# The last two table products made unit by unit, with a new order for the first stage

## The chip, the cores and the metric

The kernel runs on one core of one Trainium2 chip. The metric is the time of one execution on the device, in microseconds (us). The time before is the median of three runs; beside it there is one execution that the hardware profiler recorded.

## The reference

The model has two kinds of layers, each used twice: a long convolution along the sequence (2048 positions, 512 channels), and an attention over 8 dilated neighbours.

```python
x = A_u
x = x + _A_ref(_layernorm(x), ...)
x = x + _B_ref(_layernorm(x), ...)
x = x + _A_ref(_layernorm(x), ...)
x = x + _B_ref(_layernorm(x), ...)

def _A_ref(u, ...):
    logdA = dt * (A_re + 1j * A_im)                      # 512 channels x 128 modes
    l = arange(L).astype(A_re.dtype)                     # the lags, 0 to 2047
    P = exp(logdA[:, :, None] * l[None, None, :])
    K = einsum("dn,dnl,dn->dl", Cc, P, dB).real          # the filter of each channel
    y = irfft(rfft(u padded) * rfft(K padded))[:L]       # the convolution, by FFT
    return y + u * Dskip
```

The change lies in the first convolution layer, where the filter K is made and the convolution is run.

## The kernel before

The first stage (`kernel_and_first_conv`) makes K without ever forming P. A power of exp(logdA) for any lag is a product of two factors, one from a table Y (20 lags) and one from a table X (32 lags, multiples of 8). TensorE contracts X against Y over the 128 modes, which gives K at all lags that are wanted. In the code the first factor of each matmul is X, with Btab beside it (the second half of the same complex product for the upper 16 lags); these are the first factor's tables.

The 512 channels are cut into 8 units of 64. The tables are made on VectorE (DVE) for one or two units at a time: `CHUNKS` says unit 0 alone, 1 alone, 2 with 3, 4 with 5, 6 alone, 7 alone. For a chunk, `table_ops` first copies a seed into Y (line 423) and into X (line 428). It then doubles the tables step by step: y0, y1, y2, a, b, d, e for Y, and x1, x2, x3, x4 for X. A step is a complex multiplication: two products (lines 467 or 469, and 476 into the scratch Tscr) and an addition (482). x4 has no addition: its second product goes to Btab, and TensorE adds it up. There is room in the tables for two units; unit u may overwrite the place of unit u - 2 when that has been contracted.

For each unit, `contract` does the rest: TensorE contracts the tables into psk (line 485), psk is cast to kq (829), TensorE selects the rows (pk, 840), and pk is cast to KT (847). Two units make one group of 128 channels (dc). `k_fft` takes KT of a group through the two steps of the Fourier transform: products with FK into ps_s and Z (874, 877), a turn of Z into zt (by DMA, line 887, or by TensorE, 910 and 914), products with C2 into xp (894), and a cast to sp_k (905). `u_fft` does the same for the input: F1 in place of FK, with sp_u as the result. A copy of sp_u with its halves swapped is made by DMA or by DVE (961). DVE multiplies sp_u by sp_k into pa (969), and TensorE goes back (vp, VT, ps_y, lines 983, 986, 1005) to X (1009). A stored sp_k goes to kt_scratch for the second convolution layer.

The order of all that work is not found at run time. The code lists the operations in a `Plan`, with a choice between ways for some (which engine evacuates a buffer, or whether a turn goes by DMA). `Plan.run` then issues them in the order of a row of numbers, `ORDERS`, one row for each of the kernel's stages. Each engine executes what it gets in that order and waits at its head; nothing overtakes. An operation's costs in the code (`pl.op("V", 2 * us, ...)`) were used to find the rows and have no effect here.

SyncE (SP) issues most DMA transfers, in order as well. Early in the stage it loads the input X, turns it by DMA into xT (line 703), from which TensorE makes gram matrices (712, 716) and DVE the layer norm (721 on), and loads the constants and weights: F (F1) for `u_fft`, FK, C2, IC, F1T, and wv and wqk for the attention layer. The mean is taken out of these weights by `centred`, through ps_wc, ps_wm and wm.

Of the kernel before, what the change touches and what calls it, by code (L numbers as in the profile page):

```python
# [231 lines left out]
def load_params(nc, pp, prm):  # L232
# [14 lines left out]

GATES = (13,)
ORDERS = [
# [106 lines left out]
def moved(pl, nc, name, us, slow, fn, *after, **needs):  # L356
    return pl.either(name, lambda: pl.op("A", us, lambda: fn(nc.scalar.copy), *after, **needs),
                     lambda: pl.op("V", slow, lambda: fn(nc.vector.tensor_copy), *after, **needs))
# [156 lines left out]
def table_ops(pl, nc, T, u, n, seeds, free, fixed, casts):  # L515
    e = T.elements

    def step(what, *after):
        out = []
        for v, m in ((u, 1), (u + 1, 1)) if n == 2 and what == "x3" else ((u, n),):  # L520
            us, key = e(m, what) / 1920 + 0.069, ("sc", v, what)
            a = pl.op("V", 2 * us + (0.06 if what in ("y1", "y2", "x1", "x2") else 0), lambda v=v, m=m: T.times(v, m, what), *after, casts[T.POWER[what]], take=[] if what == "x4" else key)
            if what != "x4":
                a = pl.op("V", us, lambda v=v, m=m: T.add(v, m, what), a, drop=key)
            out.append(a)
        return out
    y = moved(pl, nc, ("seed", u), 0.15 + 0.1 * n, 0.08 + 0.066 * n, lambda copy: T.seed(copy, u, n), seeds, free)
    x = moved(pl, nc, ("second", u), 0.15 + 0.1 * n, 0.08 + 0.066 * n, lambda copy: T.second(copy, u, n), casts[3], free)
    for what in ("y0", "y1", "y2", "a", "b", "d", "e"):
        y = step(what, y)  # L530
    x = step("x1", x, fixed)
    for what in ("x2", "x3", "x4"):
        x = step(what, x)
    return [y, x]


def vt(n):
# [222 lines left out]
def kernel_and_first_conv(nc, tc, C, prm, x2d, const, kt_dram, eps, Wt):  # L760
    with ExitStack() as es:
# [4 lines left out]
        T = Tables(nc, tc, es, M)  # L766
# [13 lines left out]
        pl = Plan(psk=2, kq=2, psA=3, Z=2, zt=3, KT=2, lk=NKT, xc=NXC, xs=NXS, lads=4, pa=2, VT=1, sc=2)  # L780
# [18 lines left out]
        box, Td, Cd, Kd, Sd, Fd, Xq, Pd, Rd = {}, {}, {}, {}, {}, {}, {}, {}, {}  # L799
# [131 lines left out]
        def u_fft(dc):  # L931
            dsl = slice(dc * DCH, (dc + 1) * DCH)
            fs = spectrum("u", dc, 0, 4, lambda j, r: [(F1[:, j, r, :], columns(X, j, dc))], lambda jq: [marks["xn", jq], L["F1"], free], None)

            def residual():
                nc.sync.dma_start(columns(X, slice(0, NJ), dc), xv[:, :, dsl])
            Rd[dc] = pl.op("S", 0.7, residual, *fs, lag=5.2)

        def k_fft(dc, b0, nb):
            c0, c1 = b0 * 32, (b0 + nb) * 32  # L940

            def mats(j, r):
                x = box.get(("KT", dc))
                todo = [(late["FK"][:, i, r, :] if x else None, x and x[:, s, c0:c1]) for s, i in pairs[j]]
                if j == 0 and r == 0:
                    todo.append((C["onesr"][:], D2[:, dc * DCH + c0:dc * DCH + c1]))
                return todo
            last = [("KT", dc)] if b0 + nb == 4 else []
            spectrum("k", dc, b0, nb, mats, lambda jq: [Rd["FK", jq], L["onesr"], L["D2"], marks["k0"], *[Kd[u] for u in range(dc * 2, dc * 2 + 2) if (u % 2) * 2 < b0 + nb]], last)
# [15 lines left out]
        def product(dc, c):  # L965
            def go():
                s, t, k = box.pop(("u", dc, c)), box.pop(("swap", dc, c)), box["k", dc, c]
                pr = box["pa", dc, c] = lp.tile([128, 2, 1024], BF, name="pa", tag="pa", bufs=2)
                nc.vector.tensor_tensor(pr[:], box["U"][:, s:t + 1:t - s], k[:].unsqueeze(1).to_broadcast([128, 2, 1024]), ALU.mult)  # L969
                box["xc"].append(s)  # L970
                box["xs"].append(t)
            return pl.op("V", 1.14, go, Sd["swap", dc, c], Pd["k", dc, c], take=[("pa", dc, c)], drop=[("xc", dc, c), ("xs", dc, c), ("lk", "kt", dc, c)])
# [100 lines left out]
        for u in range(8):  # L1073
            for u0, n in CHUNKS:
                if u0 == u:
                    o = table_ops(pl, nc, T, u0, n, marks["seeds"], [Cd[x - 2] for x in range(u0, u0 + n) if x > 1], marks["fixed"], marks["casts"])
                    for x in range(u0, u0 + n):
                        Td[x] = o
            contract(u)
            dc = u // 2  # L1080
            if dc == 3:
                k_fft(3, u % 2 * 2, 2)
            elif u % 2:
                k_fft(dc, 0, 4)
            if u % 2:
                for c in range(4):
                    inverse(dc, c, product(dc, c))
                final(dc, 4 if dc == 3 else 8)
                if dc < 3:
                    u_fft(dc + 1)  # L1090
# [912 lines left out]
```

## Time and profile before

| | |
|---|---|
| median of 3 runs | 422.04 us (421.99 to 422.74) |
| the profiled execution, its time | 420.84 us |
| its span in the profile | 419.1 us |
| DVE busy over the span | 390.4 us (93%) |
| PE (TensorE) busy over the span | 354.5 us (85%) |
| ACT (ScalarE) busy over the span | 325.5 us (78%) |
| first stage, to the last X written back | 160.1 us |

All times in rows of the timeline are us from the span's start: first the start, then the duration, the engine, the line, the operation, output<-inputs with shapes, and in brackets the idle time before it with what ended it. A row with x2 or more merges instructions that follow each other; the next row's start minus this row's start is what an instruction costs an engine that is never idle. A row of waits has the total, the number of times, and the longest. DVE is VectorE, ACT is ScalarE, PE is TensorE's matmuls, PEld its weight loads.

### The profile page before, as it was taken

The page shows a single profiled execution, that of the slowest core. Times are in us where ns is not written, and L with a number is a line of the kernel's source. Part 1 is how long each engine was busy: PE and PEld are TensorE (multiplying, and loading weights), DVE is VectorE, ACT ScalarE, POOL GpSimd, SP SyncE. Part 2 cuts the span into 40 slices and gives each one's busy share as a digit, 9 for nine tenths or more (in the row PEclk, how much of TensorE's full clock was granted, in tenths as well). Part 3 has the DMA queues.
Part 4 walks back from the last instruction along what each step waited for, and adds up shares of the span by engine and source line. Part 5 has one row for each costly group of instructions (what it writes and reads, how often), then busy time and mean ns, then how long its engine had stood idle before and what let it go on. Part 6 is the DMA issues. An engine that isn't in the chain of part 4 may idle for free. (4 is left out here: it accounts for less than half of the span.)

```text
span 419.1 us, 13750 instructions
## 1 busy us (share of the span) xinstructions
PE 354.5 (85%) x5906; PEld 226.5 (54%) x5906; DVE 390.4 (93%) x643; ACT 325.5 (78%) x534; POOL 29.0 (7%) x99
## 2 busy tenths in 40 slices
PE   1367777887999989999975999899999999966995
PEld 1342555665787865446642444678864456632452
DVE  6999999799999897989999999999999999999994
ACT  6899999899899964678964589999966788762630
POOL 2000000000000200010100203020000010000321
PEclk9998899999999999999999899999999999995899
DMA  7998447987869977002334277799951000352396
GB/s 216 199 207 290 168 82 123 170 180 155 179 140 161 206 165 120 19 2 70 88 92 88 49 163 159 156 178 186 208 112 40 20 0 2 89 134 56 50 180 139
DMA packets 104914, 52.80 MB, mean 126 GB/s; under 512 B 84043, under 2 KB 96476, under 8 KB 104598
## 3 DMA queue, kind: packets, MB, share of 16 engines
q1 hardware_dynamic: 99014, 45.24, 49.9%
q0 software_dynamic: 3376, 5.37, 6.6%
q10 hardware_dynamic: 2464, 1.31, 1.1%
q8 instruction: 46, 0.75, 0.8%
q14 instruction: 14, 0.11, 0.1%
HBM read 19.30 MB, written 6.29 MB: 61 GB/s over the span
## 5 line engine op out<-in xcount | busy, mean ns | idle before, releaser
L1706 DVE TENSOR_TENSOR prod<-VX,L 128x512 bf16<-128x512 bf16 (+2 forms) x72 | 75.4, 1099 | 0.8 <-DMA VX<-VX 0.3
L1530 DVE TENSOR_TENSOR prod<-qT,kT 128x4096 bf16<-128x4096 bf16 (+1 forms) x40 | 72.3, 1855 | 0.5 <-ACT kT L1436 0.3
L877 ACT CAST Z<-ps_s 128x1024 bf16<-128x1024 f32 (+1 forms) x36 | 32.6, 944 | 1.5 <-PE ps_s L874 1.4
L1818 PE MATMUL ps_o<-wo_t,oT 128*32 128x512 bf16 x512 | 33.6, 395 | 0.0
L1485 PE MATMUL ps_v<-wv,U 128*128 128x256 bf16 x256 | 31.6, 272 | 1.7 <-ACT VX L1496 1.0
L1431 PE MATMUL ps_qk<-U,wqk 128*128 128x512 bf16 x128 | 30.3, 380 | 0.7 <-ACT qT L1436 0.7
L1496 ACT ACTIVATE VX<-ps_v,rs 128x256 bf16<-128x256 f32 x64 | 26.7, 471 | 3.8 <-PE ps_v L1485 3.0
L1485 PEld LDWEIGHTS <-U 128*128 128x128 bf16 x256 | 24.5, 97 | 9.6 <-issue 5.1
L1450 PE MATMUL ps_qk<-U,wqk 128*128 128x512 bf16 x128 | 28.8, 379 | 0.8 <-ACT X L1212 0.8
L1541 PE MATMUL Lp<-prod,sb_bones 128*32 128x512 bf16 x256 | 22.4, 412 | 5.7 <-DVE prod L1530 5.7
L1748 ACT CAST ot<-po 128x1024 bf16<-128x1024 f32 (+1 forms) x15 | 14.4, 985 | 14.3 <-PE po L1721 10.8
L1721 PE MATMUL po<-prod,sb_ident 32*32 32x512 bf16 x768 | 17.1, 428 | 7.7 <-DVE prod L1706 7.5
L969 DVE TENSOR_TENSOR pa<-sp_u,sp_k 128x2048 bf16<-128x2048 bf16 x16 | 19.2, 1221 | 4.0 <-ACT sp_k L905 2.8
L894 PE MATMUL xp<-zt,sb_C 128*128 128x512 bf16 x64 | 18.8, 379 | 4.7 <-ACT zt L914 2.2
L1818 PEld LDWEIGHTS <-oT 128*32 128x32 bf16 x512 | 13.3, 100 | 14.2 <-issue 3.8
L1431 PEld LDWEIGHTS <-wqk 128*128 128x128 bf16 x128 | 11.8, 98 | 17.0 <-issue 4.8
L1450 PEld LDWEIGHTS <-wqk 128*128 128x128 bf16 x128 | 12.4, 98 | 15.2 <-issue 1.1
L874 PE MATMUL ps_s<-KT,FK 128*128 128x128 bf16 (+1 forms) x360 | 18.9, 209 | 1.5 <-ACT KT L847 1.1
L1174 DVE TENSOR_TENSOR pa<-xc,Kt 128x2048 bf16<-128x2048 bf16 x16 | 18.9, 1217 | 0.6 <-PE vp L1186 0.3
L874 PEld LDWEIGHTS <-FK 128*128 128x128 bf16 x360 | 17.3, 98 | 3.3 <-issue 2.2
L905 ACT CAST sp_k<-xp 128x1024 bf16<-128x1024 f32 x16 | 16.2, 1029 | 2.3 <-PE xp L894 1.7
L983 PE MATMUL vp<-sb_IC,pa 128*128 128x128 bf16 x256 | 16.8, 219 | 1.4 <-ACT sp_k L905 0.7
(231 smaller groups left out, 862.4 us busy)
## 6 DMA issues: line engine op xcount, KB each, us to landing
kt_scratch<-sp_k SPq DMA_DIRECT2D x16, 256.0 KB, 3.1
Kt<-kt_scratch POOLq DMA_DIRECT2D x16, 256.0 KB, 5.9
sp_u<-sp_u SPq DMA_DIRECT2D x22, 128.0 KB, 3.2
X<-in_A_u_dram SPq DMA_DIRECT2D x8, 256.0 KB, 6.3
X<-in_A_u_dram SPq DMA_DIRECT2D x4, 512.0 KB, 5.2
Kt<-kt_scratch SPq DMA_DIRECT2D x8, 256.0 KB, 4.3
VX<-VX SPq DMA_DIRECT2D x4, 448.0 KB, 3.9
VX<-VX SPq DMA_DIRECT2D x4, 336.0 KB, 3.4
```

What stands on the lines that cost most here:

```text
L874: nc.tensor.matmul(ps[:, r, 0:n // 4, jj * 4:(jj + 1) * 4], w, x, start=(k == 0), stop=(k == len(todo) - 1))
L877: nc.scalar.copy(box["Z", kind, dc, b0][:, 0:n // 4, :, jq * 16:(jq + 1) * 16].rearrange("p g r k -> p r g k"), box.pop(("s1", kind, dc, j ...
L969: nc.vector.tensor_tensor(pr[:], box["U"][:, s:t + 1:t - s], k[:].unsqueeze(1).to_broadcast([128, 2, 1024]), ALU.mult)
L1174: nc.vector.tensor_tensor(pr[:], x[:].unsqueeze(1).to_broadcast([128, 2, 1024]), box.pop(("kt", dc, c))[:], ALU.mult)
L1431: nc.tensor.matmul(ps[:], wqk[:, ct, f0:f0 + 128], XT[:, ct // 2, 4 * s:4 * s + 4, ct % 2, :], start=(ct == 0), stop=(ct == 3))
L1450: nc.tensor.matmul(box[name][:, k * 512:k * 512 + 512], wqk[:, ct, f0:f0 + 128], XT[:, ct // 2, 4 * s:4 * s + 4, ct % 2, :], start=(ct == ...
L1485: nc.tensor.matmul(ps[:, jj].rearrange("p t h d -> p (t h d)"), XT[:, ct // 2, j + jj, ct % 2, :], wv[:, ct, fp * 256:(fp + 1) * 256], sta ...
L1496: nc.scalar.activation(out, ps, ACT.Identity, scale=r)
L1530: nc.vector.tensor_tensor(pr[:], windows(q, 0, 2), windows(kT[fp][:, a:a + n2, col(w):col(w) + 1024], -DIL * 128, 2), ALU.mult)
L1541: nc.tensor.matmul(Lp[r0:r0 + 32, w // 4, :], bones[:, w % 4 + k, :], pr[:, k, f2 - a, hb * 512:(hb + 1) * 512], start=(n == 1 and k == 0) ...
L1706: nc.vector.tensor_tensor(p2[:].rearrange("p w j t d h -> p w (j t) d h"), windows(v, -DIL * 256, taps), l.to_broadcast([128, taps, nj * 2 ...
L1818: nc.tensor.matmul(ps[r:r + 32], lhsT, rhs, start=(ft == -1 or ft == 0 and not res), stop=(ft == 3), skip_group_check=True)
```

## The change

In `table_ops`, x4 of a chunk of two units was one step of two instructions. It is now a step for each unit, x3 and x4 of a unit as a pair (x3 was made unit by unit before, too). A unit's contraction then waits for its own x4 alone, and no longer for that of its neighbour; it still waits for the Y table of both. The number of operations in the plan changes, and the order of the first stage is a new row, found by a search.

```diff
-    def step(what, *after):
-        out = []
-        for v, m in ((u, 1), (u + 1, 1)) if n == 2 and what == "x3" else ((u, n),):
-            us, key = e(m, what) / 1920 + 0.069, ("sc", v, what)
-            a = pl.op("V", 2 * us + (0.06 if what in ("y1", "y2", "x1", "x2") else 0), lambda v=v, m=m: T.times(v, m, what), *after, casts[T.POWER[what]], take=[] if what == "x4" else key)
-            if what != "x4":
-                a = pl.op("V", us, lambda v=v, m=m: T.add(v, m, what), a, drop=key)
-            out.append(a)
-        return out
+    def step(v, n, what, *after):
+        us, key = e(n, what) / 1920 + 0.069, ("sc", v, what)
+        extra = 0.06 if what in ("y1", "y2", "x1", "x2") else 0
+        a = pl.op("V", 2 * us + extra, lambda: T.times(v, n, what), *after, casts[T.POWER[what]], take=[] if what == "x4" else key)
+        return a if what == "x4" else pl.op("V", us, lambda: T.add(v, n, what), a, drop=key)
...
     for what in ("y0", "y1", "y2", "a", "b", "d", "e"):
-        y = step(what, y)
-    x = step("x1", x, fixed)
-    for what in ("x2", "x3", "x4"):
-        x = step(what, x)
-    return [y, x]
+        y = step(u, n, what, y)
+    for what in ("x1", "x2"):
+        x = step(u, n, what, x, fixed if what == "x1" else [])
+    return [[y, step(v, 1, "x4", step(v, 1, "x3", x))] for v in range(u, u + n)]
...
                     for x in range(u0, u0 + n):
-                        Td[x] = o
+                        Td[x] = o[x - u0]
```

Of the order's row only the first numbers:

```diff
-    "1 3 7 2 8 5 9 10 19 24 11 14 30 12 13 34 31 35 45 49 20 21 25 26 28 23 38 166 239 39 47 42 55 160 48 56 67 57 59 61 "
+    "242 1 3 2 7 8 9 24 25 164 26 5 10 11 162 12 236 14 27 13 19 30 20 31 21 34 35 45 23 47 48 67 42 38 49 59 68 43 166 "
```

In the row of the attention stage one number (52) moves four places on; no engine's instructions come in another order by it.

The new row also takes other ways for some operations of the first stage. DVE's instructions in the kernel go from 645 to 652: four more for x4; one more normalisation of X (4 for 3), two more seeds of Y (one of 256 elements, one of 128), one kq cast, and one more swap (two copies); one quad step (`stepped`, now four ACTIVATEs on ACT), one MYB (now on ACT) and one write-back of X (now on ACT) fewer. ACT gives up one normalisation, two seeds and one kq cast.

Lines after line 528 have numbers that are 5 lower in the new kernel. Three places follow, before and after each.

DVE at the end of the tables of units 2 and 3, before:

```order
L476 TENSOR_TENSOR Tscr<-Ytab,MSB 128x512
L469 TENSOR_TENSOR Xtab<-Xtab,MSA 128x128x32
L476 TENSOR_TENSOR Btab<-Xtab,MSB 128x4096
L482 TENSOR_TENSOR Ytab<-Ytab,Tscr 128x64x2x4
L969 TENSOR_TENSOR pa<-sp_u,sp_k 128x2048 x2
L961 COPY sp_u<-sp_u 64x1024 x2
L428 COPY Xtab<-MX_73 128x128x2
```

The same place after:

```order
L476 TENSOR_TENSOR Btab<-Xtab,MSB 128x2048
L482 TENSOR_TENSOR Ytab<-Ytab,Tscr 128x64x2x4
L469 TENSOR_TENSOR Xtab<-Xtab,MSA 128x64x32
L476 TENSOR_TENSOR Btab<-Xtab,MSB 128x2048
L956 COPY sp_u<-sp_u 64x1024 x2
L824 CAST kq<-psk 128x40x8
L964 TENSOR_TENSOR pa<-sp_u,sp_k 128x2048 x2
L423 COPY Ytab<-cb_91 128x64x4
L428 COPY Xtab<-MX_73 128x128x2
```

The two Btab rows are the two units' x4. The swap of sp_u moved ahead of pa, and a kq cast and a seed were added on DVE.

ACT around the first casts of sp_k, before:

```order
L905 CAST sp_u<-xp 128x1024
L914 COPY zt<-pt 128x1024 x2
L905 CAST sp_k<-xp 128x1024 x2
L829 CAST kq<-psk 128x40x8 x2
L905 CAST sp_u<-xp 128x1024
L829 CAST kq<-psk 128x40x8
L905 CAST sp_k<-xp 128x1024
```

The same place after:

```order
L900 CAST sp_u<-xp 128x1024
L909 COPY zt<-pt 128x1024 x2
L824 CAST kq<-psk 128x40x8
L900 CAST sp_k<-xp 128x1024 x2
L900 CAST sp_u<-xp 128x1024
L900 CAST sp_k<-xp 128x1024
L824 CAST kq<-psk 128x40x8 x2
```

The first kq cast (unit 2) moved ahead of the first sp_k.

SP's queue from the last turns of X to the weights (c_F is the constant F1), before:

```order
L703 DMA_TRANSPOSE xT<-X 128x8x128 x2
L144 DMA sb_ident<-c_ident 128x128
L703 DMA_TRANSPOSE xT<-X 128x8x128
L1068 DMA wv<-in_B_wqkv_dram 128x4x512
L144 DMA sb_C_155<-c_C 128x128
L144 DMA sb_onesr<-c_onesr 2x128
L144 DMA sb_F_153<-c_F 128x4096
L1068 DMA wqk<-in_B_wqkv_dram 128x4x1024
```

The same place after:

```order
L698 DMA_TRANSPOSE xT<-X 128x8x128 x3
L144 DMA sb_F_153<-c_F 128x4096
L698 DMA_TRANSPOSE xT<-X 128x8x128
L144 DMA sb_IC<-c_IC 128x256
L698 DMA_TRANSPOSE xT<-X 128x8x128 x2
L144 DMA sb_F1T<-c_F1T 128x4096
L1063 DMA wv<-in_B_wqkv_dram 128x4x512
L1063 DMA wqk<-in_B_wqkv_dram 128x4x1024
```

F moved ahead of the last three turns, and F1T, which was issued after FK, ahead of both weights.

46 rows, old and new, of the table ORDERS are left out of this document.

## The prediction

> **What bounds the kernel now.** The order table that is new belongs to the first stage, so I read that stage alone: first the busy time by stretches (0 to 160.1 us ends with the last X written back), then VectorE's (DVE's) waits from 60 to 160 us, then its timeline. Columns of the stretches: length, then busy time of PE, PEld, DVE, ACT, POOL, the granted clock, DMA share, GB/s.
>
> ```profile
> 0.00:75.00 75.00, 44.46 (x949) 30.61 (x950) 70.72 (x164) 69.05 (x103) 2.12 (x11) 0.95 0.74 183
> 75.00:105.00 30.00, 25.11 (x605) 19.88 (x604) 27.03 (x47) 27.62 (x36) 0.00 (x0) 1.00 0.83 169
> 105.00:136.50 31.50, 30.11 (x922) 24.93 (x919) 29.46 (x79) 28.68 (x42) 0.00 (x0) 1.00 0.81 158
> 136.50:160.10 23.60, 21.07 (x439) 16.90 (x434) 19.72 (x29) 19.01 (x26) 2.10 (x4) 1.00 0.79 178
> ```
>
> DVE is busy 147 of 160 us and ACT 144. Both run in order, so the stage lasts about DVE's work plus what DVE waits. Those waits are few:
>
> ```profile
> DVE pa L969 <- ACT sp_k L905: 2.8, 2, 2.6
> DVE Xtab L428 <- PE psk L485: 0.7, 2, 0.5
> DVE pa L969 <- PE vp L983: 0.6, 1, 0.6
> DVE Ytab L423 <- PE psk L485: 0.3, 1, 0.3
> ```
>
> The largest is behind the x4 product of units 2 and 3:
>
> ```profile
> 70.17 2.28 DVE L469 TENSOR_TENSOR Xtab<-Xtab,MSA 128x4096 bf16<-128x4096 bf16 x1
> 72.37 2.28 DVE L476 TENSOR_TENSOR Btab<-Xtab,MSB 128x4096 bf16<-128x4096 bf16 x1
> 74.57 0.42 DVE L482 TENSOR_TENSOR Ytab<-Ytab,Tscr 128x512 bf16<-128x512 bf16 x1
> 77.57 2.36 DVE L969 TENSOR_TENSOR pa<-sp_u,sp_k 128x2048 bf16<-128x2048 bf16 x2 [2.58 <-ACT sp_k L905]
> 79.97 0.86 DVE L961 COPY sp_u<-sp_u 64x1024 bf16<-64x1024 bf16 x2
> 81.03 0.30 DVE L428 COPY Xtab<-MX 128x256 bf16<-128x256 bf16 x1 [0.21 <-PE psk L485]
> ...
> 135.29 1.22 DVE L476 TENSOR_TENSOR Btab<-Xtab,MSB 128x2048 bf16<-128x2048 bf16 x1
> ```
>
> DVE has nothing in hand from 74.99 to 77.57: the product pa needs sp_k, and the next tables need the contraction (psk) of both units. Unit 7's table is ready at 136.51, and 23.6 us of chain follow it.
>
> **The change part by part: work.** x4 for two units at once is two instructions of 4096 elements. Split, it is four of 2048, as units 0 and 1 have it now:
>
> ```profile
> 42.87 1.22 DVE L469 TENSOR_TENSOR Xtab<-Xtab,MSA 128x2048 bf16<-128x2048 bf16 x1
> 44.00 1.22 DVE L476 TENSOR_TENSOR Btab<-Xtab,MSB 128x2048 bf16<-128x2048 bf16 x1
> 45.14 0.28 DVE L482 TENSOR_TENSOR Ytab<-Ytab,Tscr 128x256 bf16<-128x256 bf16 x1
> ```
>
> Start to start, 2048 elements take 1.135 us and 4096 take 2.20, so 8 x 1.135 - 4 x 2.20 = +0.28 us. The other moves between engines are priced by these rows (the second fence is ACT's):
>
> ```profile
> 11.19 1.29 DVE L551 TENSOR_TENSOR quad<-t,dtf 128x512 f32<-128x512 f32 x2
> 13.01 0.42 DVE L642 TENSOR_SCALAR MYB<-LAM 128x512 bf16<-128x512 f32 x1
> 13.34 0.69 DVE L682 TENSOR_TENSOR lads<-sq 128x512 f32<-128x512 f32 x1
> ...
> 50.63 0.40 DVE L229 TENSOR_SCALAR X<-X,ln_rstd_a,ln_nb_a 128x512 bf16<-128x512 bf16 x1
> 50.95 0.45 DVE L847 CAST KT<-pk 128x288 bf16<-128x288 f32 x1
> 51.32 0.40 DVE L229 TENSOR_SCALAR X<-X,ln_rstd_a,ln_nb_a 128x512 bf16<-128x512 bf16 x1
> ...
> 150.91 1.23 DVE L1009 CAST X<-ps_y 128x1024 bf16<-128x1024 f32 x1
> ```
>
> ```profile
> 3.44 1.28 ACT L568 ACTIVATE e_mag<-raw_A_re,dtf 128x128 f32<-128x128 bf16 x4
> ...
> 9.11 0.58 ACT L610 COPY LAM<-ptq 128x512 f32<-128x512 f32 x1 [1.41 <-PE ptq L603]
> ...
> 13.76 0.58 ACT L616 CAST cb<-ptq 128x512 bf16<-128x512 f32 x1 [1.60 <-PE ptq L603]
> ```
>
> Ahead of unit 7's table DVE loses one quad step (-0.61) and one MYB (-0.33), and gains one normalisation (+0.32), the seeds and one kq cast. The trace has no kq cast on DVE: KT, 288 elements instead of 320, takes 0.37 start to start and a 512-element pass 0.6 (quad), so I take +0.41, near KT. One more seed of 128 elements and one of 256 are bounded by nothing and 0.30 each (row 81.03); I take 0.32 together. With the split: +0.39. ACT takes the quad step as four ACTIVATEs, 1.28 by the e_mag row. They lie in the 1.41 it waits before LAM, and since this quad is ready sooner, the 1.60 before cb goes too.
>
> **Dependent pairs.** The order also decides whether an instruction follows directly on the one whose output it reads:
>
> ```profile
> 108.54 0.22 DVE L476 TENSOR_TENSOR Tscr<-Ytab,MYB 128x128 bf16<-128x128 bf16 x1
> 108.79 0.23 DVE L482 TENSOR_TENSOR Ytab<-Ytab,Tscr 128x128 bf16<-128x128 bf16 x1
> ...
> 117.90 0.22 DVE L476 TENSOR_TENSOR Tscr<-Ytab,MYB 128x128 bf16<-128x128 bf16 x1
> 118.03 0.42 DVE L482 TENSOR_TENSOR Ytab<-Ytab,Tscr 128x512 bf16<-128x512 bf16 x1
> ```
>
> The same product lets its own addition start after 0.25 us (108.54), but an addition of another step after 0.13 (117.90). I count 20 direct product-to-addition pairs and 14 addition-to-product pairs before, 11 and 13 in the new order: 10 fewer at 0.11 to 0.12, -1.1 us (none to -1.2). The Trainium skill, "VectorE: DVE Perf Modes", section "The DRAIN you can't avoid", says that the pipe empties after every operation and that waits between chained operations cost nothing extra. By it this term would be 0 and the sum below 1.1 us worse; the rows above disagree with it. Work in all: 0.39 - 1.1 = -0.7 us at unit 7's table.
>
> **Waits.** Before, DVE waits 2.58 and 0.21 in the rows above and 0.47 (0.7 less 0.21), 0.3 and 0.6 by the table: 4.2 us that the new order can reach. In the new order x4 of unit 2 ends some 2.3 us before that of unit 3, PE contracts unit 2 meanwhile, and DVE has a swap (0.86) and the kq cast (0.41) ahead of pa. But pa still needs sp_k:
>
> ```profile
> 72.99 1.95 ACT L914 COPY zt<-pt 128x1024 bf16<-128x1024 bf16 x2
> 75.61 1.93 ACT L905 CAST sp_k<-xp 128x1024 bf16<-128x1024 f32 x2 [0.68 <-PE xp L894]
> ```
>
> ACT gets there 1.2 us sooner: the early waits of 1.41 and 1.60 end, less 1.8 of work taken over (the quad step's 1.28 and 0.5 for MYB, near cb's 0.58). The new kq cast on ACT stands ahead of sp_k and waits for unit 2's contraction, which PE starts after its xp: that gives half of it back, and pa starts near 77.0. I leave 1.2 of the 2.58 in place. The rest, with the contraction of unit 3 some 2 us earlier and unit 6's table seeds no longer behind both contractions, should go: -2.7 us (bounds 0 and -4.2).
>
> **New waits.** SP's loads are rearranged: F (1 MB) now goes ahead of the last three transposes of X, and F1T (1 MB) ahead of the weights wv and wqk. PE works in order, so behind wqk's product ps_wm stands the first contraction, and behind that DVE's first KT:
>
> ```profile
> 30.24 0.30 PE L716 MATMUL gram<-xT 128*32 128x32 bf16 x16
> 37.76 1.02 PE L1024 MATMUL ps_wm<-wqk,mones 128*128 128x512 bf16 x4 [2.84 <-DMA wqk<-in_B_wqkv_dram]
> 45.48 1.01 PE L485 MATMUL psk<-Ytab,Xtab 128*64 128x40 bf16 x32 [0.65 <-DVE Ytab L482]
> ```
>
> ```profile
> 33.59 0.68 DVE L721 TENSOR_TENSOR own<-gram,sb_block 128x512 f32<-128x512 f32 x1
> ```
>
> ```profile
> 22.00:24.00 2.00, 0.00 (x0) 0.00 (x0) 2.00 (x8) 2.00 (x4) 0.00 (x0) 1.00 0.89 70
> ...
> 32.00:34.00 2.00, 2.00 (x6) 0.74 (x5) 2.00 (x7) 2.00 (x4) 0.00 (x0) 1.00 1.01 370
> ```
>
> A megabyte at 370 GB/s is 2.8 us. The gram ends at 30.5 and DVE takes it at 33.59, so that cover is 3 us, or 2 with DVE a microsecond ahead: F costs 0 to 0.8. From wqk's landing (37.7) to KT (50.95) are 13.2 us, only 0.65 of them the wait above, so a delay of wqk shows at KT nearly in full. From 22 to 24 us the DMA engines move only 70 GB/s, room that F would use, so I expect wqk within half a microsecond of now: +0.3 (0 to 3.5).
>
> **Tail.** Behind unit 7's table DVE loses an X write-back (-1.15) and gains a swap (+0.86); ACT gains the write-back late in the chain (0.97, as the sp_k cast of the same size). I take +0.5 (0 to 1.3).
>
> Sum: -0.7 - 2.7 + 0.3 + 0.5 = **-2.6 us**. From 160 us on no engine's order differs, so it should arrive whole. The profiled execution took 420.84 (span 419.1); 418.24 follows. The median, 422.04, lies 1.20 above it: **419.4**.
>
> **Rivals.**
> 1. *The weights come late: slower.* If F finds no room, wqk lands 2.8 us later, at 40.5, and KT follows 12.5 to 13.2 us on, at 53.0 to 53.7, while DVE, 0.7 us ahead, asks for it near 50.3. DVE then stands 2.7 to 3.4 us, and the gram adds up to 0.8. With 3.4 + 0.8 for the 0.3 the sum is +1.3: 423.3. It turns slower once the early stall passes 2.9 us. For it: the share of 1.01 in the row at 32 us. Against: the 70 GB/s of the row at 22. The Trainium skill, "DMA: Bandwidth & Descriptors", section "Queues, rings and completion order", has descriptors of a ring consumed in order, which speaks for the transposes waiting behind all of F; no run here shows it yet. Chance 0.14.
> 2. *The wait is only renamed.* kq on ACT holds sp_k, DVE stands at its own kq cast, pa starts at 77.6 or after, and the later waits stay by half: -0.7 - 1.3 + 0.3 + 0.5 = -1.2, 420.8. For it: PE's contraction stands behind an xp that waits for ACT. Chance 0.14.
> 3. *ACT becomes the bound.* ACT takes over the quad step, MYB and an X write-back (1.28 + 0.5 + 0.97) and gives up a normalisation, seeds and a kq cast (some 1.5): 1.2 us more, at 144 busy of 160. If its other 16 us, spent waiting, shrink by no more than that, the end stays: 422.0. Chance 0.10.
>
> **Chances and range.** My forecast has the remaining 0.62. A measurement tells 0.2%, 0.84 us, from no change. Faster: 0.62 + 0.14 = 0.76; within: 0.07 of rival 3; slower: 0.14 + 0.03 = 0.17. The range runs from the full waits and no new ones (-0.7 - 4.2 = -4.9, 417.2) to most of rival 1 (+1.0, 423.0).
>
> **What would show it.** Right: the wait of pa on sp_k near 76 us under 1.5 us, tables of units 4 and 5 begun by 79.9, unit 7's Btab done by 133.5, X written back by 157.5, and later stages shifted alike. Wrong: DVE idle at "own" or at the first KT, PE's wait for wqk above 3.9 us, sp_k later than 75.6, or ACT busy without gaps after 136 us.

## The result, and the profile after

| | before | changed | ratio, 95% interval |
|---|---|---|---|
| median, 17 runs of each | 421.99 us | 419.37 us | 0.9935, 0.9916 to 0.9953 |
| again, beside later experiments, 11 and 6 runs | 421.62 us | 419.55 us | 0.9948, 0.9928 to 0.9968 |
| profiled execution: span | 419.1 us | 417.4 us | |
| unit 7's table done (DVE) | 136.51 us | 133.16 us | |
| last X written back (ACT) | 160.08 us | 157.74 us | |

The changed kernel is 2.6 us faster in the medians. In the two profiled executions 3.35 us are won by the end of unit 7's table and 1.0 is given back in the 24 us behind it, which leaves 2.34 at the last X; the whole spans differ by 1.7. The stretches of the changed kernel, in the same columns as before (length, busy time of PE, PEld, DVE, ACT, POOL, clock, DMA share, GB/s):

```profile
0.00:75.00 75.00, 42.77 (x996) 30.02 (x998) 70.41 (x166) 70.03 (x106) 2.12 (x11) 1.00 0.80 185
75.00:105.00 30.00, 25.96 (x696) 20.95 (x687) 28.28 (x53) 28.42 (x38) 0.00 (x0) 1.00 0.92 168
105.00:136.50 31.50, 30.35 (x897) 24.65 (x894) 30.96 (x81) 28.96 (x42) 0.00 (x0) 1.00 1.06 168
136.50:160.10 23.60, 20.84 (x345) 16.30 (x345) 17.93 (x29) 18.15 (x23) 2.30 (x4) 1.00 0.85 165
```

From 75 to 136.5 us DVE has 2.26 us idle in these rows where it had 5.01. Its waits up to 139 us, from the table of waits (total, times, longest):

```profile
DVE kq L824 <- PE psk L485: 1.2, 1, 1.2
DVE KT L842 <- PE pk L835: 0.7, 1, 0.7
...
DVE Ytab L469 <- ACT Ytab L423: 0.2, 1, 0.2
```

The wait of 2.58 us for sp_k is gone from the list. In its place stands one of 1.17 us at the kq cast, which is new on DVE. DVE's timeline around it, and at unit 6 and unit 7:

```profile
73.78 1.22 DVE L476 TENSOR_TENSOR Btab<-Xtab,MSB 128x2048 bf16<-128x2048 bf16 x1
75.03 0.86 DVE L956 COPY sp_u<-sp_u 64x1024 bf16<-64x1024 bf16 x2
77.06 0.49 DVE L824 CAST kq<-psk 128x320 bf16<-128x320 f32 x1 [1.17 <-PE psk L485]
77.47 2.35 DVE L964 TENSOR_TENSOR pa<-sp_u,sp_k 128x2048 bf16<-128x2048 bf16 x2
79.97 0.23 DVE L423 COPY Ytab<-cb 128x256 bf16<-128x256 bf16 x1
...
104.74 0.23 DVE L469 TENSOR_TENSOR Ytab<-Ytab,MYA 128x128 bf16<-128x128 bf16 x1 [0.15 <-ACT Ytab L423]
...
130.88 1.22 DVE L476 TENSOR_TENSOR Btab<-Xtab,MSB 128x2048 bf16<-128x2048 bf16 x1
132.87 0.29 DVE L482 TENSOR_TENSOR Ytab<-Ytab,Tscr 128x256 bf16<-128x256 bf16 x1
```

pa starts at 77.47, hardly before the old 77.57. But the swap (0.86 us), which stood behind it before, is done by then, so the tables of units 4 and 5 begin on DVE at 79.97 where they began at 81.03. ScalarE's (ACT's) side of the same place, and its last write-back:

```profile
72.58 1.93 ACT L909 COPY zt<-pt 128x1024 bf16<-128x1024 bf16 x2
75.40 0.43 ACT L824 CAST kq<-psk 128x320 bf16<-128x320 f32 x1 [0.89 <-PE psk L485]
75.94 1.93 ACT L900 CAST sp_k<-xp 128x1024 bf16<-128x1024 f32 x2
...
155.17 2.57 ACT L1004 CAST X<-ps_y 128x512 bf16<-128x512 f32 x4 [0.69 <-PE ps_y L1000]
```

sp_k comes at 75.94, no earlier than before (75.61): ACT is only 0.4 us ahead at zt, and its own new kq cast stands first.

### The profile page after: what moved, and what is told of

Read it like the earlier page. It is cut to its first block, busy times and chain, and to the rows that moved or that the text cites. A ratio compares the mean times of both kernels' runs of the same rounds, so it can differ in the third digit from the quotient of the medians.

```text
span 417.4 us, 13763 instructions
## 1 busy us (share of the span) xinstructions
PE 351.0 (84%) x5906; PEld 225.2 (54%) x5906; DVE 389.9 (93%) x650; ACT 326.7 (78%) x536; POOL 29.2 (7%) x99
## 5 line engine op out<-in xcount | busy, mean ns | idle before, releaser
L1701 DVE TENSOR_TENSOR prod<-VX,L 128x512 bf16<-128x512 bf16 (+2 forms) x72 | 75.6, 1100 | 0.7 <-DVE L L1670 0.2
L200 DVE BATCH_NORM_STATS2 ln_st_a<-X 128x6 f32<-128x512 bf16 x24 | 15.8, 681 | 2.2 <-ACT X L1004 1.6
```

Source lines behind the costliest of these rows:

```text
L1701: nc.vector.tensor_tensor(p2[:].rearrange("p w j t d h -> p w (j t) d h"), windows(v, -DIL * 256, taps), l.to_broadcast([128, taps, nj * 2 ...
```

## The experiments

The kernels keep the changed kernel's line numbers; each ratio is to the kernel before, run in turn with it on the same chip. Where a kernel differs only by the order table, the diff shows rows of an engine's order.

### The split, with and without the new order

**joined** makes x4 for two units at once again, within the new order:

```
-... lambda: T.times(v, n, what), ...
+... lambda: T.times(v, 2 if what == "x4" and v in (2, 4) else n, what) if what != "x4" or v not in (3, 5) else None, ...
```

> The changed kernel with x4 of units 2 and 3, and of 4 and 5, made as two instructions of 4096 again, in the first unit's place and with the last Y addition ahead of them; no other instruction moves. My theory: the split pays only because a unit's contraction starts under the next unit's x4. Joined, DVE saves 0.28 us of work; the contraction of unit 2 comes some 0.6 later (74.2 to 74.8), so the kq cast on DVE waits 1.7 in place of 1.2; the contraction of unit 4 comes 1 us later (102.1 to 103.1), and unit 6's first table step, which needs it, waits some 1.5 us where it now waits 0.15. Against the changed kernel +1.5 us (0.7 to 2.0): 420.9, a ratio of 0.997 to the kernel before. Rival (the order alone makes the gain, the split only costs its work): -0.3 us, 419.1, ratio 0.993.

Measured: 420.75 us (11 runs), ratio 0.9987 (0.9974 to 1.0): 2.2 us behind the changed kernel's 0.9935, a little above the range. The two waits that the theory named came, each smaller than forecast (1.4 for 1.7, 1.0 for 1.5), and one of 0.9 for a vp beside them. DVE's waits and one row of TensorE's timeline, which now waits in the middle of unit 2's contraction:

```profile
DVE kq L824 <- PE psk L485: 1.4, 1, 1.4
DVE Ytab L469 <- ACT Ytab L423: 1.0, 1, 1.0
...
DVE pa L964 <- PE vp L978: 0.9, 1, 0.9
...
74.51 0.57 PE L485 MATMUL psk<-Ytab,Btab 128*32 128x40 bf16 x32 [0.85 <-DVE Btab L476]
```

**split_old** is the other half: the old order, with each joint x4 replaced on the spot by two single ones.

```
 DVE:
-L469 TENSOR_TENSOR Xtab<-Xtab,MSA (4096 elements), L476 TENSOR_TENSOR Btab<-Xtab,MSB (4096)
+L469 (2048), L476 (2048) of the first unit, then L469 (2048), L476 (2048) of the second
```

> The kernel before with x4 of units 2 and 3, and of 4 and 5, made unit by unit in the place of the joint instructions, with the order otherwise as before. My theory: the split alone is only its work, +0.28 us, since the last Y addition, which the contraction also needs, stays behind both halves: 422.0 to 422.3 against 421.6 to 422.0, ratio 1.0005 to 1.001. Rival (the first unit's contraction starts earlier anyhow): -0.5 us or more, ratio 0.9985.

Measured: 421.93 us (11 runs), ratio 0.9999 (0.9987 to 1.0012); pa still waits for sp_k:

```profile
77.52 2.36 DVE L964 TENSOR_TENSOR pa<-sp_u,sp_k 128x2048 bf16<-128x2048 bf16 x2 [2.40 <-ACT sp_k L900]
```

So the split alone brings nothing, and the new order without it loses nearly all of its gain (0.9987 where it had 0.9935). For this order they work only together: it starts a unit's contraction under the next unit's x4 (the changed kernel's TensorE contracts unit 2 from 74.17, while DVE makes x4 of unit 3 until 75.00). Whether a search that keeps the joint x4 would find an order as good was not tried.

### Dependent pairs

**pairs** keeps every instruction and puts each addition of the tables directly behind its product, as here at unit 6 on DVE:

```
 L476 TENSOR_TENSOR Tscr<-Ytab,MYB 128x128
+L482 TENSOR_TENSOR Ytab<-Ytab,Tscr
 L467 TENSOR_TENSOR Xtab<-Xtab,MXA x2
 L476 TENSOR_TENSOR Tscr<-Xtab,MXB 128x256
-L482 TENSOR_TENSOR Ytab<-Ytab,Tscr
 L482 TENSOR_TENSOR Xtab<-Xtab,Tscr
```

> The changed kernel with every addition of the tables put directly behind the product that it reads on DVE: 62 direct product-to-addition pairs where it has 11, the same instructions otherwise. My theory (a direct pair costs 0.11 to 0.12 us): DVE's work grows by 51 x 0.115 = 5.9 us up to unit 7's table, nearly all of it on the path: 424.5 to 425.5, slower than the kernel before (ratio 1.006 to 1.008). Rival (the Trainium skill, VectorE: DVE Perf Modes, the section on the DRAIN: every operation empties the pipe, so a dependent one costs no more): 0 us, 419.4, ratio 0.9935.

Measured: 423.38 us (5 runs), ratio 1.0049 (1.0037 to 1.0062). Rows of its DVE timeline, a product and its addition each:

```profile
108.08 0.22 DVE L476 TENSOR_TENSOR Tscr<-Ytab,MYB 128x128 bf16<-128x128 bf16 x1
108.33 0.23 DVE L482 TENSOR_TENSOR Ytab<-Ytab,Tscr 128x128 bf16<-128x128 bf16 x1
...
116.07 0.42 DVE L476 TENSOR_TENSOR Tscr<-Ytab,MSB 128x512 bf16<-128x512 bf16 x1
116.52 0.42 DVE L482 TENSOR_TENSOR Ytab<-Ytab,Tscr 128x512 bf16<-128x512 bf16 x1
...
137.74 0.29 DVE L482 TENSOR_TENSOR Ytab<-Ytab,Tscr 128x256 bf16<-128x256 bf16 x1
```

128 elements start 0.25 us after the product and 512 elements 0.45, where the changed kernel's independent ones take 0.135 and 0.335. Unit 7's table ends at 138.03, 4.87 us later, although 1.1 us less is waited (the kq cast's 1.17 and unit 6's 0.15 are gone, 0.18 is new): about 6.0 us of work for 51 more pairs, 0.117 each. The theory's price for a pair holds. Its forecast for the end, 1.006 to 1.008, was too high: of the 6 us the end shows 4.8 (1.0049 less 0.9935), since DVE comes later to its waits and finds them shorter.

### Fronts and tails of the old order

**early_old** takes the old order up to x4 of unit 2, **tail_old** takes it from unit 7's finished table on.

```
 early_old:  [order before, up to x4 of unit 2]  + [changed order, what is left]
 tail_old:   [changed order, up to unit 7's last table step] + [order before, what is left]
```

> The order and the choice of engines of the kernel before up to the x4 product of units 2 and 3 (about 70 us), and those of the changed kernel from there. The prediction's sum has nearly all of the gain behind this point: DVE reached it at 70.17 before and 70.04 after. My theory: 419.3 to 419.9, ratio 0.9935 to 0.995. Rival (the waits behind 70 us depend on what the front does for ScalarE and the loads, so without the new front the wait at pa stays): 420.5 to 422, ratio 0.9965 to 1.0.

> The changed kernel up to unit 7's last table step, and from there the order and the choice of engines of the kernel before (its swaps by DMA, an X write-back on DVE, its order of products). My theory: the new tail is longer by itself, 24.6 us from the finished table to the last X write-back where the old one took 23.6, so the old tail gives back 0.5 to 1.0 us: 418.4 to 418.9, ratio 0.991 to 0.9925. Rival (the old tail was only fast because more had been finished before it began; what the new table order leaves undone has to be done anyway): 0 to +1 us, 419.4 to 420.4, ratio 0.9935 to 0.996.

Measured: 425.41 us (6 runs), ratio 1.0078 (1.0056 to 1.0099), and 424.65 us (6 runs), 1.0072 (1.0055 to 1.0089). No theory had either number, and the traces show both failing at the joint. As these rows read, a swap by DMA waits on the issuing queue until a product frees its slot, and the transposes that ScalarE and TensorE wait for stand behind it; in early_old they go out at 81.11 where the changed kernel's go out at 74.31. First SP's queue, ACT and DVE in early_old (DVE's row names no releaser), then SP's queue and TensorE in tail_old:

```profile
79.27 1.73 SPq L956 DMA_DIRECT2D sp_u<-sp_u  x2
81.11 2.75 SPq L882 DMA_TRANSPOSE zt<-Z  x2
...
86.31 1.93 ACT L872 CAST Z<-ps_s 128x1024 bf16<-128x1024 f32 x2 [5.39 <-DMA zt<-Z]
...
93.57 1.23 DVE L964 TENSOR_TENSOR pa<-sp_u,sp_k 128x2048 bf16<-128x2048 bf16 x1 [4.86 <-issue]
```

```profile
128.75 5.29 SPq L956 DMA_DIRECT2D sp_u<-sp_u  x4
134.14 3.65 SPq L882 DMA_TRANSPOSE zt<-Z  x2
...
138.49 0.61 PE L889 MATMUL xp<-zt,sb_C 128*128 128x512 bf16 x1 [4.34 <-DMA zt<-Z]
```

So these two say nothing on the front's or the tail's own price: in both, joining two orders made a new queue jam at the seam.

### The moved loads

**loads_old** puts the two loads back, **f1t_old** only the second. SP's order, - the changed kernel, + loads_old:

```
-L698 DMA_TRANSPOSE xT<-X 128x8x128 x3
-L144 DMA sb_F_153<-c_F 128x4096
-L698 DMA_TRANSPOSE xT<-X 128x8x128
+L698 DMA_TRANSPOSE xT<-X 128x8x128 x4
 L144 DMA sb_IC<-c_IC 128x256
 L698 DMA_TRANSPOSE xT<-X 128x8x128 x2
-L144 DMA sb_F1T<-c_F1T 128x4096
 L1063 DMA wv<-in_B_wqkv_dram 128x4x512
+L144 DMA sb_F_153<-c_F 128x4096
 L1063 DMA wqk<-in_B_wqkv_dram 128x4x1024
 ...
+L144 DMA sb_F1T<-c_F1T 128x4096
```

> The changed kernel with its two moved loads back where the kernel before has them: F behind the weights wv, F1T behind the FK tables; nothing else moves. The prediction's term for the moved loads was +0.3 us (0 to 3.5). Revised theory after the trace of after: wv lands some 5 us later than before, TensorE waits 2.8 us for it and then runs wv's products slower (1.91 us for four where later ones take 1.03), ScalarE waits 1.2 us at 42 to 44 us for them, and that lateness of ScalarE is what DVE meets at the kq cast at 77 us. Then the loads put back bring 0.5 to 1.0 us: 418.4 to 418.9, ratio 0.991 to 0.9925. Rival (the cover hides them, as DVE's KT without a wait says): no change, 419.4, ratio 0.9935.

> The changed kernel with F1T alone put back behind the FK tables; F stays ahead of the last three transposes. If it is wv's lateness that costs, F1T is most of it (a megabyte, 2.8 us at 370 GB/s, directly ahead of wv): -0.4 to -0.8 us, 418.6 to 419.0, ratio 0.9915 to 0.993. If it is the gram's lateness (F ahead of its transposes), nothing comes back here and all of it with both loads put back: 419.4, ratio 0.9935. Rival to both: hidden, 419.4.

Measured: loads_old 417.71 us (5 runs), ratio 0.9905 (0.989 to 0.9919); f1t_old 419.20 us (6 runs), 0.9935 (0.9921 to 0.995). The first was run again beside the changed kernel:

> The changed kernel with F and F1T put back behind wv and FK, once more, beside the changed kernel itself. If the moved loads cost about 1.2 us, as the first run of it says (0.9905 against 0.9935): ratio 0.990 to 0.992, 1.0 to 1.3 us below the changed kernel, with no wait over 0.3 us at the kq cast near 76 us. Rival (that run was a lucky one, since two kernels that also have the loads put back came to 0.9935): within 0.4 us of the changed kernel.

> The changed kernel once more, on the same chip as the next one, as its yardstick: ratio 0.9935 within its interval, 0.9916 to 0.9953. With the loads as they are, DVE should again wait 1 us or more at the kq cast near 76 us, and ScalarE about 1 us between 40 and 60 us.

Measured: 418.10 us (6 runs), 0.9927 (0.99 to 0.9954), beside 419.55 us (6 runs), 0.9948 (0.9928 to 0.9968). These two intervals overlap. Taking both measurements together, each time divided by the median of the kernel before beside it, 11 times with the loads back have the median 0.9911 and 23 of the changed kernel 0.9942; resampling both sets puts the difference at 0.08 to 0.45%, that is 0.3 to 1.9 us, 1.3 in the middle. What the traces show, first TensorE and ACT of the changed kernel:

```profile
36.05 0.58 PE L1050 MATMUL ps_wc<-wv,sb_ident 128*128 128x512 bf16 x1 [2.82 <-DMA wv<-in_B_wqkv_dram]
36.43 1.91 PE L1052 MATMUL ps_wc<-wv,mones 128*128 128x512 bf16 x4
...
42.21 1.03 PE L1052 MATMUL ps_wc<-wv,mones 128*128 128x512 bf16 x4
...
42.20 0.59 ACT L1036 CAST wm<-ps_wm 128x512 bf16<-128x512 f32 x1 [0.31 <-PE ps_wm L1019]
44.35 1.01 ACT L1055 CAST wv<-ps_wc 128x1024 bf16<-128x1024 f32 x1 [0.86 <-PE ps_wc L1052]
```

and the kq cast on DVE, in loads_old, its second run, the changed kernel's second run, f1t_old, and last tail_old (whose loads and order are the changed kernel's up to there), with ACT's zt and sp_k ahead of it:

```profile
75.98 0.49 DVE L824 CAST kq<-psk 128x320 bf16<-128x320 f32 x1 [0.22 <-PE psk L485]
...
75.92 0.49 DVE L824 CAST kq<-psk 128x320 bf16<-128x320 f32 x1
...
77.03 0.49 DVE L824 CAST kq<-psk 128x320 bf16<-128x320 f32 x1 [1.01 <-PE psk L485]
...
77.07 0.49 DVE L824 CAST kq<-psk 128x320 bf16<-128x320 f32 x1 [1.41 <-PE psk L485]
...
71.22 1.95 ACT L909 COPY zt<-pt 128x1024 bf16<-128x1024 bf16 x2
74.59 1.93 ACT L900 CAST sp_k<-xp 128x1024 bf16<-128x1024 f32 x2
75.72 0.49 DVE L824 CAST kq<-psk 128x320 bf16<-128x320 f32 x1
```

With the loads back DVE comes through 1.1 us sooner. But in tail_old it comes through as early with the loads forward, although wv's products start there as late as 34.96 (f1t_old: 32.12); ACT does not wait there for any of them. The revised theory, that it is wv's lateness, fits the changed kernel's first trace, and these two speak against it as the whole cause: in f1t_old wv's products had no wait, and the time did not move. What f1t_old's trace has instead is a slow contraction, which ACT's next table seed waits for (f1t_old, then the same contraction in loads_old):

```profile
51.74 1.04 PE L485 MATMUL psk<-Ytab,Xtab 128*64 128x40 bf16 x32
52.71 0.72 PE L485 MATMUL psk<-Ytab,Btab 128*32 128x40 bf16 x32
53.47 0.41 ACT L423 COPY Ytab<-cb 128x256 bf16<-128x256 bf16 x1 [0.99 <-PE psk L485]
...
51.47 0.69 PE L485 MATMUL psk<-Ytab,Xtab 128*64 128x40 bf16 x32
52.09 0.57 PE L485 MATMUL psk<-Ytab,Btab 128*32 128x40 bf16 x32
52.70 0.40 ACT L423 COPY Ytab<-cb 128x256 bf16<-128x256 bf16 x1
```

The two direct measurements favour both loads back, by 0.3 to 1.9 us; with F1T alone nothing shows. The gain is not secured beyond that: the two kernels of the next part that also have both loads back came to 0.9936 and 0.9935, whether or not their own edits cost something, and unit 7's table ends at 132.18 and 133.62 in the two traces with the loads back, at 133.16 and 133.81 in those of the changed kernel and at 131.78 in tail_old. Through which delay of ACT the loads act, if they do, and whether F alone does it, stays open.

### The tail

Three kernels move work behind unit 7's table. **tail_first** (on the changed kernel) and **vp_late** (on loads_old) let the contraction go first:

```
 PE, both:   -vp of the third group's first part ahead of unit 7's contraction;  +behind its selection pk
 DVE, both:  -cast VT of that vp ahead of KT;  +behind KT
 DVE, tail_first alone:  -pa of that part ahead of unit 7's x4;  +behind unit 7's last addition
```

> The changed kernel with the product pa of the third channel group's first part, its inverse vp and the cast to VT moved behind unit 7's table, contraction and KT; nothing else moves. If the chain contraction, kq, KT sets the end of the stage: the contraction starts at 132.5 where it now starts at 133.4, KT follows at about 136.1 (137.0 now), the last X write-back 0.5 to 0.9 earlier: 418.6, ratio 0.9915. Rival (DVE and ACT set the end by the work that they have left): no change or up to 0.5 us slower, 419.4 to 419.9, ratio 0.9935 to 0.995.

> The changed kernel with the two loads put back, and with TensorE's inverse vp of the third group's first part behind unit 7's contraction and selection, its cast to VT behind KT; DVE's product stays where it is. If the head of the stage's last chain is TensorE (unit 7's table is ready at 131.9 there, its contraction starts at 132.9): the contraction starts near 132.1 and the last X write-back comes 0.4 to 0.8 us earlier, 417.0 to 417.3, ratio 0.9885 to 0.9895. Rival (ScalarE and the transposes through the DMA queue behind KT set the end): 0 to +0.5 us, ratio 0.9905 to 0.992.

Measured: 419.94 us (12 runs), ratio 0.9967 (0.9947 to 0.9987), and 418.85 us (6 runs), 0.9936 (0.9919 to 0.9954). Neither gained. In tail_first the contraction did not come sooner: it starts at 134.66, behind other products of TensorE, where the changed kernel's starts at 133.38, so that run does not test the chain. vp_late does: its contraction starts at 133.22, right behind the table. In vp_late the table ends at 133.17 and X is written back at 158.48, 25.3 us later, no shorter than the 25.1 of loads_old. **end_split** (on loads_old) turns to the other end of the tail:

```
 DVE:  -pa of the last group's fourth part, then of its third    +third, then fourth
 ACT:  -L981 CAST VT of the fourth part, 1024 elements           +512 elements on ACT and 512 on DVE
```

> The changed kernel with the two loads put back, and at the end of the stage the product of the last group's third part ahead of that of its fourth (DVE waits 0.44 us for sp_k of the fourth while the third is ready), and the last cast to VT shared by ScalarE and DVE. If the stage's end is set by the chain pa, vp, VT, ps_y behind the last two products, as the trace reads (ScalarE casts VT without a gap from 150.3 to 154.0, ps_y waits 0.88 us for it): 0.5 to 0.9 us less than with the loads alone, 416.8 to 417.2 where that kernel had 417.7, ratio 0.9885 to 0.9895. Rival (ScalarE's X write-back ahead of it or TensorE's vp sets the end): 0 to 0.2 us, ratio 0.990 to 0.9905.

Measured: 418.67 us (6 runs), ratio 0.9935 (0.9916 to 0.9955), a miss. DVE's half did not run beside ACT's but waited for it, and the pa that was to start sooner waited for a vp:

```profile
149.43 2.49 DVE L964 TENSOR_TENSOR pa<-sp_u,sp_k 128x2048 bf16<-128x2048 bf16 x2 [0.34 <-PE vp L978]
...
153.70 0.69 DVE L981 CAST VT<-vp 128x512 bf16<-128x512 f32 x1 [1.18 <-ACT VT L981]
```

The best version that was run is loads_old, below both kernels: 0.9905 and 0.9927 of the kernel before, and by 0.3 to 1.9 us below the changed kernel.

## Why the prediction was right, and where its steps were off

**The sum.** Forecast -2.6 us and 419.4, measured -2.6 and 419.37. That the two agree so closely is luck: the 17 times of the changed kernel run from 417.49 to 421.58, and the interval of the ratio allows 2.0 to 3.5 us. At unit 7's table it was -0.7 - 2.7 + 0.3 = -3.1 against -3.35 measured, and the tail +0.5 against +1.0, so two errors also offset each other.

**Work, -0.7.** DVE's waits between 60 and 136.5 us fell from 4.2 to 1.4 us, which leaves 0.55 of the 3.35 to work and early waits, forecast 0.7 - 0.3 = 0.4. The pairs' price, the larger part of it, is shown by itself: 0.117 us a pair, 1.2 us for ten. The rule of the Trainium skill, "VectorE: DVE Perf Modes", "The DRAIN you can't avoid", under which the pairs kernel would have stayed at 419.4, does not hold for these instructions.

**Waits, -2.7.** Right in size (2.8), wrong in one step. "ACT gets there 1.2 us sooner" did not happen in the profiled execution: sp_k came at 75.94 and not before 75.6, one of the signs that the prediction had named as wrong, and pa at 77.47 and not near 77.0. In tail_old, with the same order and the same loads up to there, it did: ACT turns zt from 71.22, 1.8 us sooner than before, sp_k comes at 74.59, and pa at 76.12 without a wait. So the step holds in one execution and fails in another. The first half of rival 2 is what one sees: kq on ACT holds sp_k, DVE stands at its own kq cast. Its second half did not follow, because DVE filled the time with the swap and the cast, and the later waits went. The 1.2 us that the prediction left in the wait are there (1.17), by luck: at this cast the four traces of this order show 1.17, 1.01, 2.58 and none, and the two with the loads back 0.22 and none.

**New early waits, +0.3.** The prediction looked for them at DVE (at own and at the first KT) and found cover there, rightly: own starts at 33.30 and KT at 50.62, both ahead of before. It did not look at ACT, the second busy engine, which waited 0.31 + 0.86 us for products of the late weights in the changed kernel's trace. That DVE met this lateness at the kq cast 33 us later is argued, not shown. By the times the two loads may be worth 0.3 to 1.9 us, so the term was perhaps too small; whatever it is, it lies in the 1.4 us of waits that are left above and must not be counted again. Rival 1 had the weights late and looked for the stall at DVE; DVE did not stand at own or KT.

**Tail, +0.5.** Measured +1.0, and 1.5 with the loads back. The tail is 25.1 us from a table at 132.18 (loads_old), 24.6 from 133.16 and 24.4 from 138.03 (pairs): part of what comes sooner is lost there. Neither its head (vp_late) nor its last casts (end_split) could be shown to set it; what does is open. ACT casts VT without a gap from 150.71 to 154.48, so rival 3 may hold for these last microseconds.

**Landmarks.** Unit 7's Btab by 133.5: 132.10. Tables of units 4 and 5 by 79.9: 79.97. X by 157.5: 157.74. The last two are late by 0.07 and 0.24. "It should arrive whole" is not seen in this pair of executions, which have 2.34 at the last X and 1.7 in their spans; the medians differ by 2.6.

## What to carry to other kernels

Ask of a new order not only whether the engine that bounds the stage waits, but whether the second busiest one does: its lateness can turn up where the two meet next. A product split in two pays only where the consumer's order lets it start on the first half, and an order and a split have to be judged together. Between short dependent vector instructions put one that does not depend on them; here that saved 0.117 us each time.

## What the runs showed of the hardware that was not expected

The wait at the kq cast differs between executions whose order up to there is identical: 1.17 and 1.01 us in the two of the changed kernel, 2.58 in tail_first, none in tail_old. A trace of one execution places such a wait; its size wants several. In the executions where it is long, ACT had waited for TensorE before 54 us, and TensorE's own speed differed: the second half of unit 1's contraction takes 0.69 + 0.57 us in the changed kernel's first trace and 1.04 + 0.72 in its second, with a granted clock of 1.00 and of 0.83, then 0.50, in the same stretch (first trace, then second):

```profile
50.00:52.00 2.00, 1.93 (x122) 1.83 (x121) 2.00 (x5) 2.00 (x4) 0.00 (x0) 1.00 0.04 8
52.00:54.00 2.00, 1.69 (x59) 1.50 (x54) 1.98 (x4) 2.00 (x5) 0.00 (x0) 1.00 0.00 0
```

```profile
50.00:52.00 2.00, 1.53 (x78) 1.45 (x80) 2.00 (x6) 2.00 (x3) 0.00 (x0) 0.83 0.04 8
52.00:54.00 2.00, 2.00 (x68) 1.91 (x63) 2.00 (x4) 1.35 (x4) 0.00 (x0) 0.50 0.00 0
```

The Trainium skill, "TensorE: Matmul & The Clock Gate", "Part 1: The HAM clock gate", describes a clock that halves after an idle window and recovers after a busy one, by a window that runs free of the kernel; that the same order met both clocks at the same place agrees with it. In the changed kernel's first trace four products that take 1.03 us elsewhere take 1.91 at 36.43 and stand beside a granted clock of 1.00, so the durations say more there than the clock's row.
